# Linear attention on one core: v beside a column of ones, 16 output tiles in PSUM, relu shared, eps by matmul, deeper buffers

## The chip, the cores and the metric

The kernel runs on one core of one Trainium2 chip. The metric is the device time of one execution in microseconds (us), taken over several executions; the profile is one execution, and its span (first to last instruction) is about 1.8 us shorter than the time of that execution. The profiled execution of the kernel before (span 207.2 us) is none of those in its table; by this rule it took about 209 us, a little more than their median. Engines are named TensorE (PE in the profile; PEld is its weight load), VectorE (DVE), ScalarE (ACT), GpSimd (POOL) and SyncE (SP, which here only issues DMA).

"Slow" is a run over 1.5% above the fastest of the same kernel.

## The reference, cut to what matters

```python
# q, k, v: [1, 32 heads, 2048, 128] bf16
phi_q = where(q > 0, q + 1, exp(q)) + 1e-6
phi_k = where(k > 0, k + 1, exp(k)) + 1e-6
kv  = einsum("bhsd,bhse->bhde", phi_k, v)       # 128 x 128 per head
z   = einsum("bhsd->bhd", phi_k)                # 128 per head
num = einsum("bhqd,bhde->bhqe", phi_q, kv)
den = einsum("bhqd,bhd->bhq", phi_q, z)[..., None] + 1e-6
return num / den
```

Both kernels use phi(x) = (min(exp(x), 1) + eps) + relu(x) and never add the two parts: each product is taken once with the first part and once with the second, and PSUM adds them up.

## The kernel before

Per head, ScalarE computes exp(k), and exp and relu of the transposed q from PSUM. VectorE computes min(exp, 1) + eps and relu for k, the same min for q, and evicts the outputs. TensorE does, in this order, the k·v block of the next head, the last four output tiles of the head before, the transposes of q, and the first twelve output tiles.

The k·v block has two products for each weight load, one with v (128 columns) and one with a column of ones (1 column) for z:

```python
for j in range(NT):                                  # 16
    for part, src in ((0, emk_sb), (1, rk_sb)):      # min(exp)+eps, relu
        pe.matmul(kv_ap, lhsT=src[:, be, j, :], rhs=v_sb[:, b_, j, :], start=first, stop=fin)
        last = pe.matmul(z_ap, lhsT=src[:, be, j, :], rhs=ones_sb[:, 0:1], start=first, stop=fin)
```

The output has room for 12 tiles in PSUM; tiles 12 to 15 reuse the places of the first ones, so they wait for the eviction of those (`S_evR0`), and VectorE evicts them separately. VectorE's order per head:

```python
for j in range(NH):
    kvs(j)                       # kv|z from PSUM to bf16
    if j + 1 < NH: emk_rk(j + 1) # min and relu of k
    if j >= 1: evacR0(j - 1)     # 12 tiles: + eps, reciprocal, multiply
    emq(j)                       # min of q
    if j >= 1: evacR1(j - 1)     # 4 tiles: + eps, reciprocal, multiply
```

Loads of q, k and v (512 KB each per head) have three buffers each, and so has the output.

## Time and profile before

| | before |
|---|---|
| time, median | 207.29 us (207.24 to 207.82, 3 runs) |
| span of the profile | 207.2 us |
| busy, 30 to 150 us: TensorE, ScalarE, VectorE | 94%, 94%, 88% |
| period per head, from VectorE's k min | 5.815 us |
| DMA rate, 30 to 150 us | 361 GB/s |

The first lines are of the page, busy time of each engine over the whole span and the number of instructions. The second fence is the windows view from 30 to 150 us; its columns are the length, then busy time and count of each engine, the granted clock of TensorE, the DMA share and GB/s.

```profile
PE 185.4 (89%) x3704; PEld 178.7 (86%) x3704; DVE 163.6 (79%) x320; ACT 175.5 (85%) x97; POOL 0.7 (0%) x7
```

```profile
30.00:150.00 120.00, 112.94 (x2319) 109.45 (x2319) 105.00 (x206) 112.58 (x63) 0.00 (x0) 1.00 1.00 361
```

Three engines are nearly full and none is completely. That is how a ring can look: engines that wait for each other in a circle. The waits view of before says who waits for whom (total us, times, longest):

```profile
DVE la_sb L344 <- PE la_ps L240: 20.3, 31, 2.0
ACT la_sb L192 <- PE la_ps L217: 16.9, 30, 2.4
...
ACT la_sb L187 <- DMA la_sb<-in_k_dram: 4.0, 2, 2.1
```

L344 is the eps addition of the last four tiles, L240 an output matmul. The compute engines' only waits for a DMA are two at the start. The chain of waits follows the ring itself; its columns are start, length and what ran:

```profile
98.00 0.69 DVE la_sb L352
98.69 0.20 DVE la_sb L318
98.89 0.60 DVE la_sb L303
99.48 0.61 DVE la_sb L305
100.10 0.05 issue
...
103.40 0.17 DVE la_sb L344
103.60 0.19 DVE la_sb L346
103.81 0.69 DVE la_sb L352
104.50 0.20 DVE la_sb L318
```

Left out between 100.15 and 103.40 is TensorE alone: the k·v block (2.60 us) and the four last output tiles. From one L352 (eviction of the four tiles) to the next it is 5.81 us: k·v block and four tiles 3.25, then VectorE's eps, reciprocal and eviction 1.10, copy of kv|z 0.20, min and relu of k 1.21. ScalarE is not in it.

### The profile page before, as it was taken

The page shows a single profiled execution, that of the slowest core. Times are in us where ns is not written, and L with a number is a line of the kernel's source. Part 1 is how long each engine was busy: PE and PEld are TensorE (multiplying, and loading weights), DVE is VectorE, ACT ScalarE, POOL GpSimd, SP SyncE. Part 2 cuts the span into 40 slices and gives each one's busy share as a digit, 9 for nine tenths or more (in the row PEclk, how much of TensorE's full clock was granted, in tenths as well). Part 3 has the DMA queues.
Part 4 walks back from the last instruction along what each step waited for, and adds up shares of the span by engine and source line. Part 5 has one row for each costly group of instructions (what it writes and reads, how often), then busy time and mean ns, then how long its engine had stood idle before and what let it go on. Part 6 is the DMA issues. An engine that isn't in the chain of part 4 may idle for free.

```text
span 207.2 us, 8114 instructions
## 1 busy us (share of the span) xinstructions
PE 185.4 (89%) x3704; PEld 178.7 (86%) x3704; DVE 163.6 (79%) x320; ACT 175.5 (85%) x97; POOL 0.7 (0%) x7
## 2 busy tenths in 40 slices
PE   6999999999999999999999999999999997989652
PEld 6999999999999999999999999999999997989541
DVE  0246888888898888888898888888899885889663
ACT  4699599999999999999999999999999996997600
POOL 1000000000000000000000000000000000000000
PEclk9999999999999999999999999999999999999975
DMA  6999799999999999999999999999999999942222
GB/s 235 388 415 407 298 313 357 357 338 342 346 370 378 398 356 337 347 353 365 350 366 359 381 399 392 393 332 338 353 348 373 345 356 365 318 172 107 104 101 101
DMA packets 18610, 67.63 MB, mean 326 GB/s; under 512 B 2064, under 2 KB 2192, under 8 KB 18576
## 3 DMA queue, kind: packets, MB, share of 16 engines
q1 hardware_dynamic: 18576, 67.12, 88.9%
q8 instruction: 29, 0.48, 0.9%
q14 instruction: 5, 0.04, 0.1%
HBM read 50.33 MB, written 16.78 MB: 324 GB/s over the span
## 4 chain that ended last, share of the span: by engine, by line
PE 57%; DVE 38%; issue 3%; POOLq 0%; POOL 0%
PE la_ps L233 41%; DVE la_sb L352 10%; DVE la_sb L305 9%; DVE la_sb L303 9%; PE la_ps L239 5%; PE la_ps L240 5%; DVE la_sb L318 3%; DVE la_sb L346 3%; DVE la_sb L344 3%; PE la_ps L267 2%; PE la_ps L271 2%; DVE la_sb L338 2%; PE la_ps L234 2%; PE la_ps L217 1%; DVE la_sb L330 0%
## 5 line engine op out<-in xcount | busy, mean ns | idle before, releaser
L233 PE MATMUL la_ps<-la_sb 128*128 128x128 bf16 x1024 | 87.8, 217 | 11.3 <-DVE la_sb L305 9.9
L233 PEld LDWEIGHTS la_ps<-la_sb 128*128 128x128 bf16 x1024 | 83.2, 96 | 15.4 <-DVE la_sb L305 15.2
L234 PE MATMUL la_ps<-la_sb 128*128 128x1 bf16 x1024 | 85.7, 164 | 0.0
L234 PEld LDWEIGHTS la_ps<-la_sb 128*128 128x128 bf16 x1024 | 83.5, 96 | 1.4 <-issue 1.4
L192 ACT ACTIVATE la_sb<-la_ps 128x2048 bf16<-128x2048 bf16 x32 | 60.0, 1877 | 16.9 <-PE la_ps L217 16.9
L239 PE MATMUL la_ps<-la_sb 128*128 128x129 bf16 x512 | 66.1, 222 | 5.0 <-DVE la_sb L338 4.6
L240 PE MATMUL la_ps<-la_sb 128*128 128x129 bf16 x512 | 66.2, 222 | 0.4 <-issue 0.4
L187 ACT ACTIVATE la_sb<-la_sb 128x2048 bf16<-128x2048 bf16 x32 | 61.2, 1913 | 4.0 <-DMA la_sb<-in_k_dram 4.0
L196 ACT ACTIVATE la_sb<-la_ps 128x2048 bf16<-128x2048 bf16 x32 | 59.9, 1872 | 0.0
L338 DVE TENSOR_TENSOR la_sb<-la_ps,la_sb 128x1536 bf16<-128x1536 f32 x32 | 56.2, 1757 | 1.3 <-DVE la_sb L330 0.2
L239 PEld LDWEIGHTS la_ps<-la_sb 128*128 128x128 bf16 x512 | 49.8, 98 | 6.2 <-DVE la_sb L338 5.1
L240 PEld LDWEIGHTS la_ps<-la_sb 128*128 128x128 bf16 x512 | 50.4, 99 | 0.0
L217 PE MATMUL la_ps<-la_sb 128*128 128x128 bf16 x512 | 33.8, 219 | 0.1
L217 PEld LDWEIGHTS la_ps<-la_sb 128*128 128x128 bf16 x512 | 29.9, 98 | 0.2 <-issue 0.2
L303 DVE TENSOR_SCALAR la_sb<-la_sb 128x2048 bf16<-128x2048 bf16 x32 | 21.9, 683 | 6.0 <-ACT la_sb L187 6.0
L352 DVE TENSOR_TENSOR la_sb<-la_ps,la_sb 128x512 bf16<-128x512 f32 x32 | 22.1, 691 | 1.1
L305 DVE TENSOR_SCALAR la_sb<-la_sb 128x2048 bf16<-128x2048 bf16 x32 | 21.9, 686 | 0.0
L312 DVE TENSOR_SCALAR la_sb<-la_sb 128x2048 bf16<-128x2048 bf16 x32 | 21.9, 683 | 0.0
L344 DVE TENSOR_SCALAR la_sb<-la_ps 128x4 f32<-128x4 f32 x32 | 5.2, 163 | 20.5 <-PE la_ps L240 20.3
L318 DVE CAST la_sb<-la_ps 128x129 bf16<-128x129 f32 x32 | 9.1, 285 | 7.8 <-PE la_ps L234 7.8
L330 DVE RECIPROCAL la_sb<-la_sb 128x12 f32<-128x12 f32 x32 | 7.3, 228 | 1.1
L328 DVE TENSOR_SCALAR la_sb<-la_ps 128x12 f32<-128x12 f32 x32 | 5.2, 164 | 2.5 <-PE la_ps L240 2.5
(13 smaller groups left out, 24.5 us busy)
## 6 DMA issues: line engine op xcount, KB each, us to landing
la_sb<-in_k_dram SPq DMA_DIRECT2D x32, 512.0 KB, 9.3
la_sb<-in_q_dram SPq DMA_DIRECT2D x32, 512.0 KB, 7.2
la_sb<-in_v_dram SPq DMA_DIRECT2D x32, 512.0 KB, 7.8
out_dram<-la_sb SPq DMA_DIRECT2D x31, 512.0 KB, 8.6
out_dram<-la_sb SPq DMA_DIRECT2D x1, 384.0 KB, 2.3
out_dram<-la_sb SPq DMA_DIRECT2D x1, 128.0 KB, 1.9
```

The source lines that it names most:

```text
L187: act.activation(ek_sb[:, be, :], k_sb[:, b_].rearrange("p j d -> p (j d)"), ACT.Exp).then_inc(S_ek, 1)
L192: act.activation(eq_sb[:, be, :], xT_ps[:, :], ACT.Exp).then_inc(S_eT, 1)
L196: act.activation(rq_sb[:, be, :], xT_ps[:, :], ACT.Relu).then_inc(S_rT, 1)
L217: last = pe.transpose(xT_ps[:, j * P:(j + 1) * P], q_sb[:, b_, j, :], ident[:])
L233: pe.matmul(kv_ap, lhsT=src[:, be, j, :], rhs=v_sb[:, b_, j, :], start=first, stop=fin)
L234: last = pe.matmul(z_ap, lhsT=src[:, be, j, :], rhs=ones_sb[:, 0:1], start=first, stop=fin)
L239: pe.matmul(o_ap, lhsT=emq_sb[:, be, tt * P:(tt + 1) * P], rhs=kvs_sb[:, be, lo:hi], start=True, stop=False)
L240: return pe.matmul(o_ap, lhsT=rq_sb[:, be, tt * P:(tt + 1) * P], rhs=kvs_sb[:, be, lo:hi], start=False, stop=True)
L303: dve.tensor_scalar(emk_sb[:, be].rearrange("p j d -> p (j d)"), ek_sb[:, be, :], 1.0, EPS, op0=ALU.min, op1=ALU.add).then_inc(S_emk, 1)
L305: dve.tensor_scalar(rk_sb[:, be].rearrange("p j d -> p (j d)"), k_sb[:, b_].rearrange("p j d -> p (j d)"), 0.0, None, op0=ALU.max).then_in ...
L338: dve.tensor_tensor(out=m_out, in0=m_in, in1=m_r, op=ALU.mult).then_inc(S_evR0, 1)
L352: dve.tensor_tensor(out=r_out, in0=r_in, in1=r_r, op=ALU.mult).then_inc(S_evR1, 1)
```

## The change

Its intent is to take work off TensorE and ScalarE and out of this ring. In parts:

1. GpSimd copies v into a buffer with 129 columns whose last column is one, so that kv and z are one product (32 matmuls of 129 columns).
2. All 16 output tiles have their own place in PSUM; kv|z has the rest of the last bank.
3. eps of the denominator comes from a small matmul that opens each bank, six per head, and VectorE's two eps additions go.
4. relu of the transposed q: in three heads of four ScalarE does one half and VectorE the other; in the fourth ScalarE does all.
5. ScalarE copies kv|z to bf16 instead of VectorE.
6. Eight load buffers instead of three, six output buffers.

The whole program was rewritten around a small class that takes each instruction with the names of those it depends on and derives the waits. Cut to its core (lines left out are marked):

```diff
-                        pe.matmul(kv_ap, lhsT=src[:, be, j, :], rhs=v_sb[:, b_, j, :], start=first, stop=fin)
-                        last = pe.matmul(z_ap, lhsT=src[:, be, j, :], rhs=ones_sb[:, 0:1], start=first, stop=fin)
+                        ins = e.matmul(kv_ps, lhsT=src[:, h % 2, j * D:(j + 1) * D], rhs=v1_sb[:, h % 2, j, :],
+                                       start=(j + part == 0), stop=(j == NT - 1 and part == 1))
 ...
+        def v1(h):
+            dep = [f"ldv{h}"]
+            if h >= 2:
+                dep += [f"kv{h - 2}"]
+            if h >= 3:
+                dep += [f"nA{h - 3}"]           # output tiles of an earlier head
+            add("POOL", f"v1{h}", lambda e: e.tensor_scalar(
+                v1_sb[:, h % 2, :, 0:D], v_sb[:, h % NI].rearrange("p (j d) -> p j d", d=D), 1.0, 0.0,
+                op0=ALU.mult, op1=ALU.add), dep)
 ...
+        def split(h):
+            return h % 4 != 3
 ...
+            e.matmul(_ap(o_ps[:, :], slot(tiles[0]) + D, [[NC, n]]), lhsT=ones[:], rhs=epsr[:, 0:n], start=True, stop=False,
+                     skip_group_check=True)
 ...
-    NBI = 3
-    NBO = 3
+    NI = 8
+    NO = 6
 ...
+        for i in range(NH):
+            eq(i)                                # ScalarE: exp of q
+            ...                                  # rqa(i): ScalarE: relu of q
+            if i + 1 < NH:
+                kvs(i + 1)                       # ScalarE: copy of kv|z
+            if i + 2 < NH:
+                ek(i + 2)                        # ScalarE: exp of k
+            if i >= 1:
+                f(i - 1, "A")                    # VectorE: 12 tiles out
+            rqb(i)                               # VectorE: half of relu of q
+            emq(i)                               # VectorE: min of q
+            if i >= 1:
+                f(i - 1, "C")                    # VectorE: 4 tiles out
+            if i + 2 < NH:
+                emrk(i + 2)                      # VectorE: min and relu of k
+            if i + 1 < NH:
+                T(i + 1)                         # TensorE: transposes of q
+            nA(i)                                # TensorE: 12 output tiles
+            nC(i)                                # TensorE: 4 output tiles
+            if i + 2 < NH:
+                kv(i + 2)                        # TensorE: k.v block
```

The comments at the right are added here. The wait of the copy of v on the output tiles of three heads ago (`nA`) is needed by no data.

## The prediction

> **What bounds it now.** The timeline shows a strict period of 5.815 us per head (VectorE's k-min at 40.65, 46.46 us ...). No engine is full: in the windows view of 30 to 150 us TensorE is 94% busy, ScalarE 94%, VectorE 88%; in the waits view no compute engine waits for a DMA after the start. The chain of waits shows a ring: TensorE's k·v block (64 matmuls, 2.60 us: each 56 ns kv product is followed by a 25 ns z product) -> the last 4 output tiles (0.45, and 0.22 drain) -> VectorE's eps add, reciprocal, 512-wide eviction (0.16, 0.18, 0.69), kv copy (0.29), min and relu of k (0.68, 0.69) -> next k·v block. Start to start: 5.8.
>
> **What the change does.**
> - kv|z as one product of 129 columns: matmuls of that shape start 57.2 ns apart, so 32 take 1.83 us instead of 2.60.
> - All 16 output tiles have PSUM: the last 4 tiles, their eviction and the eps adds leave this ring. Six tiny matmuls are added (0.2 us, off the ring).
> - The kv copy moves to ScalarE (estimate 0.28 us, from 1877 ns for 2048); half of relu(qT) goes to VectorE in 3 heads of 4. ScalarE falls from 5.4 to about 5.0 us per head; VectorE stays near 5.1.
> - GpSimd copies v, 2048 elements. The Trainium skill (GPSIMD Engine Reference, section 4.1) calls one-input operations there roughly line rate; at its stated 1.2 GHz that gives an estimate of 1.7 us, say 2.2 with overhead; the trace has nothing comparable.
> - No load is waited for now; deep buffers only protect.
>
> **New ring.** k·v(h) -> kv copy (ScalarE) -> exp k(h+1), issued after it -> min, relu (VectorE) -> k·v(h+1). With trace durations: 2.00 (with drain) + 0.18 + 1.91 + 0.61 + 0.69 and four hops of about 0.05 = 5.55 us. Most of what TensorE saves does not arrive: exp k now stands in the ring. Gain 0.26 us per head, 7.5 us over 28 heads. A recurrence over all waits also gives 5.55. The start loses about 1 us (v lands third, then GpSimd's copy); the end gains 2 to 3. Sum about 198.
>
> **DMA.** 2.1 MB per 5.55 us is 378 GB/s; load-only slices reach 415, and eight heads of lead cover a deficit. Not binding.
>
> **Predicted: 198.5 us, 8 in 10 between 193.5 and 206. Faster by over 2%: 0.86; within 2%: 0.09; slower: 0.05.**
>
> **Right if** the profile shows: k·v block about 1.85 us; period 5.5 to 5.65; a chain of waits alternating TensorE k·v, ScalarE exp k, VectorE min/relu; TensorE busy falling to about 85%; VectorE's min/relu at their old duration.
>
> **Wrong if:** (1) GpSimd's copy takes over 2.6 us. The Trainium skill (SBUF — State Buffer, "Who interferes with whom") says GpSimd shares a port pair with VectorE's two-port modes and the loser blocks for the whole instruction. The added wait on the output tiles puts the copy beside the PSUM evictions, a window of 2.0 to 2.6 us before the next min; a longer copy, or one slipping in before the k relu, delays the ring by the excess; 3.5 us would make the kernel slower. (2) VectorE's PSUM relu costs the 1.03 ns per element of the fp32 PSUM copy (1.2 us instead of about 0.65): VectorE then binds, near 205. (3) Mixed loads and stores cannot pass about 360 GB/s: load waits would appear late.

## The result, and the profile after

| | before | after |
|---|---|---|
| time, median | 207.56 us (207.24 to 208.58, 4 runs) | 199.61 us (199.09 to 203.12, 4 runs) |
| span of the profile | 207.2 us | 197.3 us |
| period per head | 5.815 us | 5.525 us |
| k·v block, start of its first product to end of its last | 2.74 us | 2.02 us |
| DMA rate, 30 to 150 us | 361 GB/s | 415 GB/s |

Ratios in this document are the mean time of one kernel's fast runs over that of the other's in the same rounds, so not quite the ratio of the medians. Here it is 0.9593 (95% interval 0.955 to 0.9636): faster by 4%. One of the four runs after (203.12 us) was slow and is left out of the ratio.

Busy time on the page, and the windows view, 30 to 150 us, of after:

```profile
PE 170.6 (86%) x2842; PEld 160.5 (81%) x2842; DVE 161.6 (82%) x254; ACT 160.0 (81%) x129; POOL 68.4 (35%) x38
```

```profile
30.00:150.00 120.00, 109.70 (x1879) 102.91 (x1880) 108.73 (x169) 108.46 (x87) 46.65 (x22) 1.00 1.03 415
```

TensorE lost 15 us of work and ScalarE 15 us, and the span fell by 10. The chain of waits of after shows the new ring (L190 exp of k, L220 and L222 min and relu of k, L251 the k·v block, L215 the copy of kv|z):

```profile
79.47 1.80 ACT la L190
...
81.29 0.70 DVE la L220
81.99 0.61 DVE la L222
...
82.65 2.04 PE la L251 x32
...
84.71 0.28 ACT la L215
84.99 1.81 ACT la L190
```

From one exp of k to the next it is 5.52 us, and in it ScalarE stands with 2.1 us (1.80 and 0.28) that the old ring did not have. The waits view of after, for comparison with that of before:

```profile
POOL la L236 <- PE la L265: 97.5, 29, 3.5
DVE la L220 <- ACT la L190: 27.4, 32, 7.1
ACT la L215 <- PE la L251: 23.0, 25, 4.0
```

GpSimd's first line costs nothing: it waits on purpose. VectorE's k min waits for exp of k, and ScalarE's copy of kv|z for the k·v block: two links of the ring.

Where the 9.9 us of span came from can be read from the starts of the k min. The fourth head's stands at 23.21 us before and 26.05 after, so the start lost 2.8 us. From there to the last head's (187.99 and 180.73) it is 164.8 and 154.7 us, a gain of 10.1. What follows is 19.2 and 16.6 us, a gain of 2.6. Of the 10.1 us, 28 times 0.29 are 8.1; the other 2.0 are two heads near the end of this one execution of before that took 7.26 and 6.33 us instead of 5.81. In the longer one TensorE stood still for 1.31 us in the middle of a k·v block, with no wait that the profile shows; why is open. So the change itself is worth 7.9 us in this account (8.1 and 2.6 less 2.8), which is what the medians say: 207.56 less 199.61.

### The profile page after: what moved, and what is told of

It is laid out like the page before. It is cut to its first block, busy times and chain, and to the rows that moved or that the text cites. A ratio compares the mean times of both kernels' runs of the same rounds, so it can differ in the third digit from the quotient of the medians.

```text
span 197.3 us, 6384 instructions
## 1 busy us (share of the span) xinstructions
PE 170.6 (86%) x2842; PEld 160.5 (81%) x2842; DVE 161.6 (82%) x254; ACT 160.0 (81%) x129; POOL 68.4 (35%) x38
## 4 chain that ended last, share of the span: by engine, by line
ACT 37%; PE 33%; DVE 22%; DMA 3%; issue 2%; POOL 1%; SPq 0%
ACT la L190 21%; PE la L251 18%; DVE la L299 9%; ACT la L202 6%; ACT la L194 6%; DVE la L220 6%; PE la L243 5%; PE la L263 5%; PE la L265 5%; DVE la L222 4%; DMA la<-in_v_dram 3%; ACT la L215 3%; DVE la L207 2%; DVE la L293 1%; POOL la L236 1%
## 5 line engine op out<-in xcount | busy, mean ns | idle before, releaser
L236 POOL TENSOR_SCALAR la<-la 128x2048 bf16<-128x2048 bf16 x32 | 67.7, 2116 | 109.1 <-PE la L265 97.5
L299 DVE TENSOR_TENSOR la<-la 128x1536 bf16<-128x1536 f32 x64 | 78.4, 1224 | 2.2
L251 PE MATMUL la<-la 128*128 128x129 bf16 x1024 | 65.3, 222 | 5.7 <-DVE la L222 5.4
L251 PEld LDWEIGHTS la<-la 128*128 128x128 bf16 x1024 | 59.7, 98 | 10.2 <-DVE la L222 7.1
L265 PE MATMUL la<-la 128*128 128x129 bf16 x512 | 66.7, 221 | 0.0
L263 PE MATMUL la<-la 128*128 128x129 bf16 x512 | 66.6, 220 | 0.0
L194 ACT ACTIVATE la<-la 128x2048 bf16<-128x2048 bf16 x32 | 59.8, 1869 | 3.7 <-PE la L243 3.7
L190 ACT ACTIVATE la<-la 128x2048 bf16<-128x2048 bf16 x32 | 60.9, 1902 | 1.9 <-DMA la<-in_k_dram 1.9
L265 PEld LDWEIGHTS la<-la 128*128 128x128 bf16 x512 | 49.8, 97 | 0.0
L263 PEld LDWEIGHTS la<-la 128*128 128x128 bf16 x512 | 47.6, 98 | 0.0
L243 PE MATMUL la<-la 128*128 128x128 bf16 x512 | 35.0, 222 | 12.7 <-DVE la L207 11.5
L220 DVE TENSOR_SCALAR la<-la 128x2048 bf16<-128x2048 bf16 x32 | 22.2, 694 | 27.4 <-ACT la L190 27.4
L243 PEld LDWEIGHTS la<-la 128*128 128x128 bf16 x512 | 29.6, 99 | 18.0 <-DVE la L207 15.5
L202 ACT ACTIVATE la<-la 128x1024 bf16<-128x1024 bf16 (+1 forms) x32 | 39.6, 1238 | 0.0
L259 PE MATMUL la<-la 128*128 128x3 bf16 (+1 forms) x192 | 32.5, 169 | 2.2 <-DVE la L227 2.2
L215 ACT ACTIVATE la<-la 128x129 bf16<-128x129 f32 x32 | 9.0, 280 | 23.0 <-PE la L251 23.0
L222 DVE TENSOR_SCALAR la<-la 128x2048 bf16<-128x2048 bf16 x32 | 22.0, 687 | 0.0
L227 DVE TENSOR_SCALAR la<-la 128x2048 bf16<-128x2048 bf16 x32 | 21.8, 683 | 0.0
L259 PEld LDWEIGHTS la<-la 128*128 128x128 bf16 x192 | 19.0, 99 | 2.4 <-DVE la L227 2.4
L207 DVE TENSOR_SCALAR la<-la 128x1024 bf16<-128x1024 bf16 x24 | 16.3, 681 | 0.0
```

What stands on the lines that cost most here:

```text
L190: add("ACT", f"ek{h}", lambda e: e.activation(em_sb[:, h % 2], k_sb[:, h % NI], ACT.Exp), [f"ldk{h}"] + ([f"kv{h - 2}"] if h >= 2 else []))
L194: add("ACT", f"eq{h}", lambda e: e.activation(emq_sb[:, h % 2], xT[:, :], ACT.Exp), [f"T{h}"] + ([f"nC{h - 2}"] if h >= 2 else []))
L202: add("ACT", f"rqa{h}", lambda e: e.activation(rq_sb[:, h % 2, 0:n], xT[:, 0:n], ACT.Relu), [f"T{h}"] + ([f"nC{h - 2}"] if h >= 2 else []))
L220: add("DVE", f"em{h}", lambda e: e.tensor_scalar(em_sb[:, s], em_sb[:, s], 1.0, EPS, op0=ALU.min, op1=ALU.add), [f"ek{h}"])
L222: add("DVE", f"rk{h}", lambda e: e.tensor_scalar(rk_sb[:, s], k_sb[:, h % NI], 0.0, None, op0=ALU.max), [f"ldk{h}"] + ([f"kv{h - 2}"] if h ...
L236: add("POOL", f"v1{h}", lambda e: e.tensor_scalar(v1_sb[:, h % 2, :, 0:D], v_sb[:, h % NI].rearrange("p (j d) -> p j d", d=D), 1.0, 0.0, o ...
```

## The experiments

All twelve kernels gave correct results. The theory to test: the ring k·v -> copy of kv|z -> exp k -> min, relu -> k·v sets the period, and the rest of the change matters only as far as it touches this ring. (The places in PSUM for all tiles and the copy of kv|z on ScalarE, parts 2 and 5, were not run alone.) The rivals: the deeper buffers and their DMA rate; the relief of ScalarE; the relief of TensorE as such. A second theory came with it: VectorE's two-port instructions and GpSimd's copy exclude each other, as the Trainium skill states (SBUF — State Buffer, "Who interferes with whom"), and the change is fast only because the copy falls beside the evictions.

### Part by part

**Three buffers (e1_buf3).**

```diff
-    NI = 8
-    NO = 6
+    NI = 3
+    NO = 3
```

> Three-head load buffers and three output buffers instead of eight and six, all else as in the changed kernel. Ring theory (k·v -> kv copy -> exp k -> min, relu -> k·v, 5.525 us per head): no load is waited for with three heads either, so within 1 us of the changed kernel's 199.6. Rival, that the deep buffers gave the gain (DMA moved 360 GB/s before and 416 GB/s after): back to about 207, with load waits on ScalarE or GpSimd.

Measured 203.81 us (201.52 to 208.35, one of four slow), ratio to before 0.976, interval 0.967 to 0.985, so by the verdict unclear at 2%. Neither expectation holds: about half of the gain is gone. The groups of this run (line, engine, instruction, shapes, count, busy us, mean ns of one, idle before it and releaser) show how:

```profile
L236 POOL TENSOR_SCALAR la<-la 128x2048 bf16<-128x2048 bf16 x32 | 61.6, 1925 | 121.4 <-DMA la<-in_v_dram 102.0 <-PE la L265 19.4
L227 DVE TENSOR_SCALAR la<-la 128x2048 bf16<-128x2048 bf16 x32 | 32.2, 1006 | 0.0
```

GpSimd now waits for its loads, no other engine does after the start, and the min of q (L227) takes 1006 ns on average where it took 683; in 12 heads of 32 its record is over 0.8 us. A late v starts GpSimd's copy at a bad moment.

**Deep buffers for v alone (e9_v_deep).** The test of that reading: three buffers for k and q, eight for v, six for the output.

```diff
-        k_sb, q_sb, v_sb = sb([P, NI, N]), sb([P, NI, N]), sb([P, NI, N])
+        k_sb, q_sb, v_sb = sb([P, NK, N]), sb([P, NK, N]), sb([P, NI, N])    # NK = 3, NI = 8
```

> The changed kernel with three-head buffers for k and q, eight for v, six for the output. The run with three of everything took 203.8 us, and its GpSimd waited 102 us for loads of v. Theory: only v needs the lead, because GpSimd copies it two heads ahead of its use and a late v starts the copy at a bad moment, so that VectorE's min of q waits for it: with v deep alone 199 to 201 us, the min of q back at 0.68 us. Rival, that three heads are too few for k and q or for the DMA rate as such: near 203.8 again.

Measured 199.78 us (198.64 to 200.85, 6 runs), ratio 0.9595, that of the changed kernel (0.9593) within its interval. The min of q is at 727 ns on average. So the lead is not needed for k and q; it is needed for v or the output, which went back to six buffers in the same kernel, so that its share is not separated. In e1 GpSimd waits for v and no engine for a store, which speaks for v. Its first use now stands one head before its k·v block (in after, a copy starts at 98.84 and its k·v block at 104.75; the text says two). The SyncE waits of e1 show a second reason why v comes late: v is issued right behind q, whose issue waits for the transposes, 90.8 us in 29 waits. Which of the two counts more was not tested.

**Deep buffers in the kernel before (e11_before_buf8).**

```diff
-    NBI = 3
-    NBO = 3
+    NBI = 8
+    NBO = 6
```

(The first loads are ordered head by head, and exp k always waits for its buffer.)

> The kernel before with eight-head load buffers and six output buffers and nothing else changed. Ring theory: no load was waited for, so 207.5 us within 1 us. Rival, that the rate of 360 GB/s held it: below 204 us.

Measured 207.08 us against 207.96 of before, ratio 0.995. The DMA rate rose to 411 GB/s (30 to 150 us) in this kernel too, without an effect over 1%: the loads only ended earlier. The rate of 361 GB/s was what the old ring asked for. (The Trainium skill, HBM Reference, section "Specifications (TRN2)", expects about 425 GB/s for a core alone; the 411 here and the 415 of after, with one store to three loads, lie near it.)

**relu wholly on ScalarE (e3_relu_act).**

```diff
         def split(h):
-            return h % 4 != 3
+            return False
```

> relu(qT) wholly on ScalarE in every head. Ring theory: ScalarE's own round (exp q, relu, kv copy, exp k: 1.77 + 1.78 + 0.18 + 1.80 = 5.53) is just as long as the ring, so 199.6 within 1 us: sharing the relu gives nothing here. Rival, that freeing ScalarE (94% to 81% busy) made the gain: at least 4 us slower.

Measured 199.51 us; the fast runs had 197.22, 199.46 and 199.55. ScalarE went from 81% to 90% busy and the time stayed. The sharing of relu gives nothing in this order of instructions. But ScalarE has no room left: from 30 to 150 us it is busy for 120.0 of 120 us, so its own round is now just as long as the ring, as expected, and this run cannot say which of the two sets the period. One of the four runs took 238.19 us at a granted clock of 0.887; more on that below.

**z as its own product (e2_z_apart).**

```diff
-                        ins = e.matmul(kv_ps, lhsT=src[...], rhs=v1_sb[:, h % 2, j, :], ...)
+                        e.matmul(kv_ps[:, 0:D], lhsT=src[...], rhs=v1_sb[:, h % 2, j, 0:D], ...)
+                        ins = e.matmul(kv_ps[:, D:NC], lhsT=src[...], rhs=ones[:, 0:1], start=False, ...)
```

> The z column as a product of its own again (64 matmuls in the k·v block). Ring theory: the block goes from about 1.83 to 2.60 us and all of the 0.77 us lands in the period, 6.29 us per head, about 223 us. Rival, that TensorE at 86% busy has room: at most 3 us slower.

Measured 273.22 us (271.97 to 274.04), ratio 1.313. Both expectations missed by far. VectorE's timeline of this run (start, length, engine, line, instruction, idle before) and GpSimd's show what happened:

```profile
99.77 0.69 DVE L220 TENSOR_SCALAR la<-la 128x2048 bf16<-128x2048 bf16 x1 [0.89 <-ACT la L190]
100.38 2.39 DVE L222 TENSOR_SCALAR la<-la 128x2048 bf16<-128x2048 bf16 x1
```

```profile
100.08 2.14 POOL L236 TENSOR_SCALAR la<-la 128x2048 bf16<-128x2048 bf16 x1 [3.57 <-PE la L268]
```

GpSimd came while the k min (99.77 to 100.46) was at work. It waited for that one instruction only and then went ahead of the k relu, which had been issued at 100.38 and now took 2.39 us instead of 0.69. The k relu is in the ring, so every such head is 1.7 us longer; 19 of the 32 heads are such. Over the run its busy time is 54.3 us instead of 22.0, which makes 32.3 of the 75 us. TensorE waits for the k relu for 48.7 us in 23 waits, and its granted clock is 0.872 on average; that the one causes the other was not tested.

**The same without GpSimd (e5_no_pool).** As e2, but the products read v from its load buffer and GpSimd does nothing.

```diff
+                        e.matmul(kv_ps[:, 0:D], lhsT=src[...], rhs=v_sb[:, h % NI, j * D:(j + 1) * D], ...)
+                        ins = e.matmul(kv_ps[:, D:NC], lhsT=src[...], rhs=ones[:, 0:1], start=False, ...)
 ...
-        for h in range(NH):
-            v1(h)
```

> GpSimd does nothing: the z column is a product of its own (against a column of ones) and kv reads v straight from its load buffer; all else as in the changed kernel. Together with the run that kept GpSimd's copy and split off z (273 us). Ring theory: without GpSimd the lock is gone, the k relu is back at 0.69 us, and only the longer k·v block (2.60 instead of 1.83 us) is left in the ring: 6.29 us per head, about 223 us. Rival, that 273 us came from the split products themselves: about 270 again.

Measured 220.83 us (220.49 to 222.3), period 6.25 us, k relu at 686 ns, clock 0.987. This is what the ring alone says: the k·v block, from the start of its first product to the end of its last, takes 2.74 us instead of 2.02, and the period is longer by the same 0.72. Between e2 and e5 the span differs by 53.4 us: 32.3 are the k relu, and the kv products are busy for 107.1 us instead of 89.0, another 18.1 (at the lower clock).

### GpSimd's moment

**The copy of v without its extra wait (e4_v1_early).**

```diff
-            if h >= 3:
-                dep += [f"nA{h - 3}"]
```

> GpSimd's copy of v no longer waits for the output tiles of three heads ago, only for its data and its buffer. Lock theory (GpSimd and VectorE's two-port min/relu exclude each other for a whole instruction): the copy moves beside VectorE's min of q and then of k, which wait for it; about 6.5 us per head by a recurrence, near 226 us, with longer VectorE min records. Rival, no such lock (only mild sharing): 199.6 within 1 us, or faster, since v is ready sooner.

Measured 224.08 us (223.95 to 224.28), ratio 1.077. The timelines of VectorE and GpSimd:

```profile
101.12 0.68 DVE L207 TENSOR_SCALAR la<-la 128x1024 bf16<-128x1024 bf16 x1
101.72 2.24 DVE L227 TENSOR_SCALAR la<-la 128x2048 bf16<-128x2048 bf16 x1
```

```profile
101.51 1.90 POOL L234 TENSOR_SCALAR la<-la 128x2048 bf16<-128x2048 bf16 x1 [4.80 <-PE la L249]
```

GpSimd started at 101.51, beside VectorE's relu from PSUM (L207), which went on at its usual 0.68 us. The min of q (L227), SBUF to SBUF, had to wait until 103.41 and took 2.24, and so in 20 heads of 32; the period is 6.7 us in three heads of four and 5.51 in the fourth. So the extra wait, which no data needs, saves 24 us. This agrees with the lock as the skill's page states it: the same section says that a VectorE instruction with at most one SBUF input, outside its two-port modes, does not contend with GpSimd. The relu from PSUM has no SBUF input; in which mode it ran the trace does not show.

**eps by VectorE (e8_eps_dve).**

```diff
-            e.matmul(_ap(o_ps[:, :], slot(tiles[0]) + D, [[NC, n]]), lhsT=ones[:], rhs=epsr[:, 0:n], start=True, ...)
 ...
+            add("DVE", f"d{which}{h}", lambda e: e.tensor_scalar(den_sb[...], ..., EPS, None, op0=ALU.add), ...)
```

> eps added by VectorE again (two small instructions per head, 0.16 us each) instead of by six small matmuls. Ring theory: VectorE has 0.3 to 0.9 us of idle per head ahead of the k min, which takes up most of the 0.4 us: 5.60 us per head, 201 to 203 us. Rival, that each VectorE instruction counts in full: 5.9 us per head, 211 us.

Measured 215.82 us; the two fast runs had 211.21 and 213.84. The number is that of the rival. But VectorE's and GpSimd's timelines say something else:

```profile
107.53 0.69 DVE L221 TENSOR_SCALAR la<-la 128x2048 bf16<-128x2048 bf16 x1 [0.49 <-ACT la L191]
108.14 2.39 DVE L223 TENSOR_SCALAR la<-la 128x2048 bf16<-128x2048 bf16 x1
...
114.77 0.68 DVE L221 TENSOR_SCALAR la<-la 128x2048 bf16<-128x2048 bf16 x1
115.37 0.68 DVE L223 TENSOR_SCALAR la<-la 128x2048 bf16<-128x2048 bf16 x1
```

```profile
108.08 1.90 POOL L237 TENSOR_SCALAR la<-la 128x2048 bf16<-128x2048 bf16 x1 [3.02 <-PE la L264]
```

GpSimd arrived at 108.08, 0.06 us before the k relu at 108.14, and won. This happens in one head of four from the tenth on, six in all: periods of 5.5 us and then one of 7.25.

**eps by VectorE, all heads alike (e10_eps_dve_relu_act).** If the collision came from the heads with the full relu, making all heads the same (as in e3, which cost nothing) should remove it. Edit: e8 and e3 together.

> eps on VectorE as in the run that took 216 us, with relu(qT) wholly on ScalarE, which alone cost nothing (199.5 us) and makes every head alike for GpSimd. Theory: the two small VectorE instructions cost next to nothing by themselves; the 216 us came from one head in four in which GpSimd took the port pair ahead of the k relu (2.39 instead of 0.69 us). So 199 to 201 us, with no k relu over 0.8 us. Rival, that the small instructions are themselves the cost: 209 us or more.

Measured 237.44 us (231.15 to 238.1); four of six runs are slow, and the two fast ones had 231.15 and 232.74. The expectation failed: now 19 heads of 32 collide, in a profile that is itself of a run labelled slow:

```profile
L223 DVE TENSOR_SCALAR la<-la 128x2048 bf16<-128x2048 bf16 x32 | 54.3, 1697 | 0.0
```

All six runs have a granted clock of 0.90 to 0.92. So making the heads alike had made it worse, and the cost of eps was still not told apart from the lock.

**The same with the copy tied to the k relu (e12_eps_guarded).** One wait differs from e10: the copy of v waits for VectorE's k relu, the instruction that it must not overtake, instead of for TensorE.

```diff
-                dep += [f"nA{h - 3}"]
+                dep += [f"rk{h - 1}"]
```

> The kernel of the 237 us run (eps on VectorE, relu(qT) wholly on ScalarE) with one wait changed: GpSimd's copy of v(h) waits for VectorE's k relu of head h-1 instead of TensorE's output tiles of head h-3, so it cannot take the port pair ahead of that relu and falls beside the 12-tile eviction. Lock theory: the k relu is 0.69 us in every head and the time returns to 199 to 202 us, eps on VectorE costing nothing that shows. Rival, that the small eps instructions or the different order of output tiles are the cost: still 209 us or more.

Measured 199.18 us (197.58 to 200.51, 6 runs), ratio 0.957. The groups of this run, and GpSimd's timeline:

```profile
L223 DVE TENSOR_SCALAR la<-la 128x2048 bf16<-128x2048 bf16 x32 | 21.9, 686 | 0.0
```

```profile
99.56 1.90 POOL L237 TENSOR_SCALAR la<-la 128x2048 bf16<-128x2048 bf16 x1 [3.63 <-DVE la L292]
```

One wait moved, and no k relu takes over 0.69 us. Fast runs against fast runs, about 232 us became 199. (The releaser is printed as L292, the next VectorE instruction; the wait is on the k relu just ahead of it.) Two things follow. eps by VectorE costs nothing that shows (e3, with the small matmuls, has 199.51), so the six small matmuls gain nothing in this ring; and the whole of the 33 us came from where the copy falls. Between the two profiles, 235.3 and 197.2 us, the k relu accounts for 32.4 of 38.1 us (54.3 less 21.9); the rest goes with a granted clock of 0.913 against 0.988. The margin is small here too: the copy ends at 101.46 and the min of q starts at 101.52.

The profiles of the changed kernel and of e3 show how near they stand to this. In every fourth head of after, GpSimd starts just behind the k relu, here at 104.06, 0.05 us after the 104.01 of the k relu, and then waits for it, so its record is 2.39 us instead of 1.90:

```profile
98.84 2.08 POOL L236 TENSOR_SCALAR la<-la 128x2048 bf16<-128x2048 bf16 x1 [3.44 <-PE la L265]
104.06 2.39 POOL L236 TENSOR_SCALAR la<-la 128x2048 bf16<-128x2048 bf16 x1 [3.13 <-PE la L265]
```

In e3 every head from the fifth on is like this. Its one run of 238 us has about the time of e10, which would fit the collision, but no profile of that run exists: this stays open, and so does the 203.12 us run of after.

### Cutting the ring

**Only exp k before the copy of kv|z (e7_ek_first).**

```diff
-            if i + 1 < NH:
-                kvs(i + 1)
             if i + 2 < NH:
                 ek(i + 2)
+            if i + 1 < NH:
+                kvs(i + 1)
```

> Only the first of those three: exp of k before the kv copy, the rest as in the changed kernel. The recurrence says that this alone is worse: kv copy and with it the next k·v and the last tiles wait for the exp, 5.98 us per head, about 211 us. Rival, that the ring is simply cut: near 190 us.

Measured 214.17 us (212.51 to 216.1), ratio 1.025, interval 1.018 to 1.032, unclear at 2%. It is slower than the changed kernel, as expected, but the profiled run, slow, also shows the lock (the k min at 1038 ns on average), so the size of the effect of the order alone is not separated.

**Three orders at once (e6_reorder).** The same, and VectorE's half of relu ahead of the 12-tile eviction, and shared in every head.

```diff
-            return h % 4 != 3
+            return True
 ...
-            if i + 1 < NH:
-                kvs(i + 1)
             if i + 2 < NH:
                 ek(i + 2)
+            if i + 1 < NH:
+                kvs(i + 1)
+            rqb(i)
             if i >= 1:
                 f(i - 1, "A")
-            rqb(i)
             emq(i)
```

> Three orders changed at once, as a recurrence over all waits picks them: ScalarE does exp of k before the kv copy (so exp of k leaves the ring), VectorE does its half of relu(qT) before the 12-tile eviction, and shares relu in every head. Ring theory: period 5.2 us (VectorE's own round, 5.17), so 189 to 192 us. Rival, that something else (DMA at 416 GB/s, or GpSimd's port) already holds 5.5 us: 199.6 or more.

Measured 188.82 us (188.48 to 189.63, 6 runs), ratio to before 0.9065: the fastest kernel, 5% below the changed one. These orders were picked by a recurrence: each instruction starts when its engine is free and its last releaser has ended plus 0.05 us, with durations from the trace and with the lock; what it gave is in the expectation, 5.2 us a head and 189 to 192 us. The chain of waits of this run, here over one head and a half, is VectorE alone:

```profile
103.52 0.68 DVE la L207
104.20 0.15 DVE la L293
...
104.37 1.76 DVE la L299
106.13 0.60 DVE la L227
...
106.85 0.69 DVE la L299
107.54 0.60 DVE la L220
108.14 0.41 DVE la L222
108.56 0.11 issue
108.66 0.68 DVE la L207
```

VectorE works without a gap, 118.4 of the 120 us from 30 to 150, and the period is its own round of 5.15 us. ScalarE is out of the chain. Here the sharing of relu is part of a version that gains; which of the three orders gives how much was not run.

## Why the prediction was right

- **The ring.** Predicted k·v, copy of kv|z, exp k, min and relu, 5.55 us; the chain of waits shows these links in this order, and the period is 5.525 us. The k·v block was predicted at 2.00 us with drain and measures 2.02. Splitting z off again without GpSimd (e5) made the block and the period longer by the same 0.72 us. Shown.
- **Busy shares.** TensorE about 85%: 86%. ScalarE about 5.0 us per head: 160.0 / 32 = 5.0. VectorE near 5.1: 161.6 / 32 = 5.05. The min and relu kept their durations (683 to 694 ns).
- **GpSimd's copy.** Estimated at 1.7, say 2.2 us; it takes 1.90 undisturbed and 2.12 with its own waiting. It fits the window, as the prediction had it, and the first of its reasons for being wrong is confirmed as a mechanism by e2, e4 and e12: a copy at the wrong moment costs 1.7 us in a head where it gets ahead of the k relu (e2), 1.2 where it gets ahead of the min of q (e4). That the changed kernel escapes this by 0.05 us in every fourth head is luck: the prediction's window was not worked out that finely, and e8 is on the other side.
- **VectorE's relu from PSUM.** 0.68 us; the 1.2 us of the second warning did not come.
- **DMA.** Mixed loads and stores ran at 415 GB/s; the third warning did not come, and e11 shows that the old 361 GB/s was no limit.
- **Sizes that were off.** The start loses 2.8 us, not 1. It was mis-sized because the exp of k of the second head, too, now stands behind the first k·v block and copy: the k min of the second head starts at 14.21 us instead of 12.30. The other 0.9 us come by the third head. There the windows view, 17.0 to 20.2 us, has a granted clock of 0.50 after and 1.00 before, and the second k·v block takes 2.53 us instead of 2.02; how much of the 0.9 us that makes, and why the clock fell, is open. The loop gained 8.1 us by its period, not 7.5 (the 10.1 of the profiles has the two long heads of before in it). The end gained 2.6, as predicted. Together 7.9 instead of about 9: hence 199.6 and not 198.5.
- **The step that failed.** "No load is waited for now; deep buffers only protect." True of the old kernel (e11), false of the new one: with three buffers everywhere it takes 203.8 us, GpSimd waits 102 us for v, and the min of q takes 1006 instead of 683 ns (e1); v's lead, with the output buffers, restores 199.8 (e9). The prediction saw that nothing waited for loads and did not ask whose first use the change moves earlier. This did not hurt the forecast, because the change brings the deep buffers with it.

## What to carry to other kernels

When no engine is full, write down the ring of waits and its terms before costing a change: here the k·v block lost 0.72 us and the last four tiles with their eviction left the ring, yet a head gained only 0.29, because exp of k, 1.80 us, had moved into it. Where GpSimd copies beside VectorE's SBUF-to-SBUF instructions, tie its start by a semaphore to the VectorE instruction that it must not overtake, not to one that happens to end about then: the same work took 199 or about 232 us. And after such a change, try the orders within each engine: with nothing added, three orders took another 5%.

## What the Trainium skill lacked or had wrong

- SBUF — State Buffer, "Who interferes with whom": the lock is as stated, and "whoever issues first" fits the cases timed here. A copy that arrives while one VectorE instruction is at work waits for it and goes ahead of the next (e2: the copy at 100.08, the k relu at 100.38, which took 2.39 us), and 0.05 to 0.06 us decide (e8 and after). The section does not say how this looks in a profile: not as idle time but as a longer record of the loser, 2.24 or 2.39 us instead of 0.68 on VectorE, 2.39 instead of 1.90 on GpSimd.
- GPSIMD Engine Reference, section 4.1 calls one-input operations "roughly line-rate", and the only elementwise duration found on that page for 2048 elements is of a two-input addition in fp32 (4497 ns). A multiply-add with constants over 128x2048 bf16 takes 1.90 us undisturbed; 2048 elements at the page's 1.2 GHz are an estimate of 1.71. (Section 3.1 of the page has a per-element model, but no duration for such an operation.)
- SBUF — State Buffer, "Summary: rules for kernel authors" advises to plan HBM transfers at about 358 GB/s; this core, alone, held 415 GB/s over 120 us with loads and stores mixed. HBM Reference has the distinction right.
